# Identity matmuls ahead of the first operands, zero fills on GpSimd, and a later table load in a one-core attention and feed-forward kernel

## The chip, the core and the metric

The kernel runs on one core of a Trainium2 chip. The metric is the device time of one execution in microseconds (us), median of several runs. TensorE does the matmuls, VectorE, ScalarE and GpSimd the work on elements, and SyncE (SP) issues the DMA transfers. Each engine runs its own queue of instructions in order and waits on semaphores for the others. In the profile PE is TensorE, PEld its weight loads, DVE is VectorE, ACT is ScalarE and POOL is GpSimd.

## What is computed

```python
# attention: batch 2, 8 heads, 768 tokens, head size 64, 16 clusters
q_assign = argmax(normalise(q) @ normalise(centroids).T)
k_assign = argmax(normalise(k) @ normalise(centroids).T)
scores = where(q_assign == k_assign, q @ k.T / sqrt(64), -1e9)
attn = softmax(scores) @ v                 # (1536, 512) after the heads are joined
# first feed-forward block, then the second
x = ((x @ w1) * (x @ w2)) @ w3 @ w_out
h = x @ w_in
out = (h * clip(h + 3, 0, 6) / 6) @ w_out2
```

## The kernel before

All operands are float32. To keep their precision on TensorE each one is split into a high part of a shorter format and a low part, and products are made of three matmuls; that is what names like `hi`, `lo`, `woh` and `wol` mean. The weights arrive as 64-bit floating-point numbers and are turned into float32 on the chip, tile by tile: a copy on ScalarE (`cvt`, line 186), a clamp (line 700, mostly on GpSimd) and three integer steps on VectorE (lines 705, 709 and 713: shift, low bits, sign) into `cvs`. From there a tile is either split into `woh` and `wol`, or transposed on TensorE (`pt`, line 731) and split into `wT` (copy on ScalarE, difference on VectorE, line 183). The matmuls `psw` (line 759) multiply weight matrices with each other while attention runs.

There are 16 heads (8 heads in 2 batches). For each head q and k are loaded, split and stacked (`qs`, `ks`), transposed on TensorE (`ptqB`, `ptkB`, line 352) and copied back (`qB`, `kB`). The centroids are normalised once at the start (`cen`, lines 262 to 297, transposed as `pc` and copied to `cT`). The matmuls `pa` (line 378) give each token's products with the 16 centroids; eight small steps (lines 393 to 406, on VectorE and GpSimd) turn them into one-hot codes `ohs`, which TensorE transposes (`pto`, line 367) and which are copied into rows 0 to 15 of `qA` and `kA`. The scores are the sum of two matmuls, `kB` with `qB` and `kA` with `qA` (`pst`, line 484), so that tokens of unlike clusters get a large negative term. Then come the row maximum (line 493), the exponential (line 501), the transposes of the probabilities (`ptr`, line 509) and the product with v (`av`, line 529).

The order on every engine is made before the program is built, by the class `Plan`. Each operation is entered with `op(name, engine, estimated time, function, needs, due=...)`. `order()` walks through them greedily: among the operations that can start soonest on an engine it takes the one that is due first, and it keeps rings of buffers (`take`, `drop`). Operations entered with `fop` have a choice of engine, and the planner gives them to the one that would end first by its estimates. So an operation that is entered, moved or given another time at the start can change the order and the engine of later ones.

At the start four buffers `qA` and `kA` are filled with zeros in rows 0 to 63 (lines 254 and 255). The identity `id_f` is made on GpSimd and cast to `id_r` on VectorE (line 258); every transpose needs one of the two. `cen_2` (line 273) does the square root for the centroids on ScalarE, and with it the one tiny activation that makes ScalarE load the table of the exponential ahead of its first use:

```python
    def cen_2():
        nc.scalar.activation(out=W_["cst"][:, 1:2], in_=W_["cst"][:, 0:1], func=AF.Sqrt)

        nc.scalar.activation(out=W_["warm"], in_=three, func=AF.Exp)
```

Of the kernel before, what the change touches and what calls it, by code (L numbers as in the profile page):

```python
# [8 lines left out]
F32 = mybir.dt.float32  # L9
# [33 lines left out]
class Plan:  # L43
# [10 lines left out]
    def op(self, key, eng, dur, fn, need=(), due=0.0, take=(), drop=(), lat=0.0, lock=False, after=()):  # L54
        assert key not in self.ops, key
        if isinstance(eng, str):
            eng, dur = (eng,), (dur,)
        self.ops[key] = [key, dict(zip(eng, dur)), None, fn, tuple(need), due, tuple(take), tuple(drop), lat,
            len(self.ops), lock, tuple(after)]
# [76 lines left out]
def cluster_attention_moe_kernel(  # L136
# [14 lines left out]
    nc = tc.nc  # L151
# [22 lines left out]
    ps_a = astk.enter_context(tc.tile_pool(name="ps_a", bufs=1, space=PSUM))  # L174
    ps_s = astk.enter_context(tc.tile_pool(name="ps_s", bufs=3, space=PSUM))

    mm = nc.tensor.matmul
# [16 lines left out]
    def blk(i):  # L194
# [15 lines left out]


    NQ, NK, NP, NO = 1, 1, 6, 1
    plan = Plan({
        "raw": 2, "rawx": 6, "cvt": 2, "cvs": 2, "hl": 2, "wT": 3, "m": 1, "s": 3, "r": 2, "a": 1, "x": 1, "x1b": 1,
        "qn": 2, "kn": 2, "vn": 1, "qs": NQ, "ks": NK, "vs": 2, "qB": 2, "kB": 2, "qA": 2, "kA": 2, "oh": NO,
# [3 lines left out]
    op = plan.op  # L219
# [31 lines left out]
    oh_ = [ar.tile([128, NC, 48], F32R, tag=f"oh{i}", name="ohs") for i in range(NO)]  # L251
    for t in oh_:
        nc.gpsimd.memset(t[:, :, NCL:32].bitcast(F32), 0.0)
    for t in (qA_[0], kA_[0], qA_[1], kA_[1]):
        nc.vector.memset(t[0:64].bitcast(F32), 0.0)
    for c in range(NCL):
        nc.gpsimd.memset(wtab[:, c:c + 1], float(NCL - c))
    op("id", "dve", 0.14, lambda: nc.vector.tensor_copy(id_r, id_f), due=-20)

    def cen_load():  # L260
# [12 lines left out]
    def cen_2():  # L273
        nc.scalar.activation(out=W_["cst"][:, 1:2], in_=W_["cst"][:, 0:1], func=AF.Sqrt)

        nc.scalar.activation(out=W_["warm"], in_=three, func=AF.Exp)

    def cen_3():
        cen, csq, cst = W_["cen"], W_["csq"], W_["cst"]
# [15 lines left out]
    def cen_T(s):  # L295
        pt = W_["pc"] = ps_m.tile([128, H, NCL], F32R, tag="m", name="pc")
        nc.tensor.transpose(
            pt.rearrange("p h c -> p (h c)"), W_["cs"][:, s].rearrange("p r d -> p (r d)"), id_r
        )
# [2 lines left out]
    op("cen1", "dve", 0.6, cen_1, ("cenl",), due=-14, take=("as1",))  # L302
    op("cen2", "act", 1.4, cen_2, ("cen1",), due=-13.9)
    op("cen3", "dve", 1.7, cen_3, ("cen2",), due=-13, take=("p",), drop=("p", "as1"))
    op(("cT", 0), "pe", 0.11, lambda: cen_T(0), ("cen3", "id"), due=-10, take=("m",))
    op(("cTc", 0), "dve", 0.2, lambda: nc.vector.tensor_copy(cT[:, :, 0, :], W_["pc"]), (("cT", 0),), due=-9.9,
        drop=("m",))
# [1107 lines left out]
```

## Time and profile before

| | |
|---|---|
| median of 3 runs | 805.14 us (804.45 to 807.4) |
| the profiled execution's own time | 804.47 us |
| its span in the profile | 802.7 us |
| TensorE busy | 770.7 us (96% of the span) |
| VectorE busy | 621.4 us (77%) |
| ScalarE busy | 506.9 us (63%) |
| GpSimd busy | 250.1 us (31%) |

The profile records one execution. Times in the timeline count from the start of the span. A row in the timeline gives the start, the time taken, the engine, the line of the kernel, the operation and its tiles; `x6` says that six like instructions that follow each other stand in one row; in brackets stands how long the engine was idle before it and whose end released it. Matmuls are pipelined, and a row of several runs from the first one's start to the last one's end.

### The profile page before, as it was taken

What the parts mean: (1) busy time and instruction counts of PE and PEld (TensorE: products, weight loads), DVE (VectorE), ACT (ScalarE), POOL (GpSimd) and SP (SyncE); (2) the same over time, 40 slices, a digit from 0 to 9 for tenths busy, and PEclk for the clock granted to TensorE, in tenths of its full rate; (3) what the DMA queues carried; (4) which work ended last, traced back from release to release, by engine and by line L of the source; (5) the groups of instructions that cost most, each with busy time, mean ns of one, the idle gap of its engine ahead of it and who ended that gap; (6) DMA issues with size and microseconds to landing.
All of it is one profiled execution on the core that took longest, in us unless ns stands there. A gap on an engine that the chain in (4) does not pass through costs nothing.

```text
span 802.7 us, 12725 instructions
## 1 busy us (share of the span) xinstructions
PE 770.7 (96%) x4498; PEld 705.8 (88%) x4498; DVE 621.4 (77%) x1095; ACT 506.9 (63%) x1008; POOL 250.1 (31%) x290
## 2 busy tenths in 40 slices
PE   4789999999999999999999999998999999999998
PEld 3677878998889999999889999997889888988986
DVE  7889888899999987788995843779966666766752
ACT  5667877787778776767744532446656557555643
POOL 5654534534355544423221422313121000200000
PEclk9989999999999999999999999999999999999999
DMA  8444333333354543422336587672211213221102
GB/s 274 127 139 127 96 110 86 86 105 110 90 182 136 162 136 109 144 84 83 125 122 186 173 286 258 185 253 96 79 60 61 92 53 132 93 64 57 50 14 78
DMA packets 53135, 98.42 MB, mean 123 GB/s; under 512 B 4848, under 2 KB 31568, under 8 KB 51536
## 3 DMA queue, kind: packets, MB, share of 16 engines
q1 hardware_dynamic: 53072, 97.62, 38.8%
q8 instruction: 35, 0.57, 0.3%
q14 instruction: 28, 0.23, 0.1%
HBM read 73.43 MB, written 17.87 MB: 114 GB/s over the span
## 4 chain that ended last, share of the span: by engine, by line
PE 79%; DVE 7%; ACT 7%; DMA 4%; issue 2%; POOL 0%; SPq 0%; ACTq 0%; DVEq 0%
PE po L1307 15%; PE psh L1263 13%; PE psab L989 8%; PE psx L938 8%; PE psab L821 7%; PE pst L484 7%; PE av L529 6%; PE ptr L509 6%; PE psw L759 4%; PE pa L378 2%; ACT p L501 1%; ACT ph L186 1%; DMA raw<-in_moe_w_dram 1%; DMA qA<-qB 1%; DVE den L493 1%
## 5 line engine op out<-in xcount | busy, mean ns | idle before, releaser
L186 ACT ACTIVATE ph<-ptr 128x384 fp32r<-128x384 f32 x192 | 90.9, 487 | 48.9 <-PE ptr L509 48.1
L183 DVE TENSOR_TENSOR pl<-ptr,ph 128x384 fp32r<-128x384 f32 x192 | 102.7, 549 | 16.3 <-ACT ph L186 15.1
L493 DVE TENSOR_REDUCE den<-pst 128x1 f32<-128x768 f32 x96 | 91.2, 950 | 10.9 <-PE pst L484 8.3
L700 POOL TENSOR_SCALAR cvt<-cvt 128x512 f32<-128x512 f32 x72 | 51.8, 720 | 144.0 <-ACT cvt L186 135.1
L501 ACT ACTIVATE p<-pst,den 128x768 f32<-128x768 f32 x96 | 86.4, 900 | 12.9 <-DVE den L493 12.4
L509 PE MATMUL ptr<-id_f,p 128*128 128x128 f32 x576 | 89.6, 276 | 1.4 <-DVE pl L183 0.7
L821 PE MATMUL psab<-xT,abhl 128*128 128x384 f32 x384 | 85.8, 347 | 0.6 <-ACT asb L186 0.6
L509 PEld LDWEIGHTS ptr<-id_f,p 128*128 128x128 f32 x576 | 69.4, 141 | 9.2 <-PE pt L731 0.9
L186 ACT ACTIVATE cvt<-raw 128x512 f32<-128x512 f32 x72 | 48.1, 669 | 44.1 <-DMA raw<-in_moe_w_out_dram 16.4
L484 PE MATMUL pst<-kB,qB 128*128 128x512 f32 x192 | 71.8, 378 | 3.4 <-ACT p L501 3.1
L529 PE MATMUL av<-ph,vs 128*128 128x384 f32 x192 | 70.2, 366 | 0.1
L529 PE MATMUL av<-pl,vs 128*128 128x384 f32 x192 | 64.9, 338 | 2.1 <-DVE pl L183 2.1
L989 PE MATMUL psab<-xT1s,abhl 128*128 128x384 f32 x384 | 66.9, 334 | 0.0
L989 PEld LDWEIGHTS psab<-xT1s,abhl 128*128 128x128 f32 x384 | 66.5, 188 | 0.2 <-ACT asb L186 0.2
L821 PEld LDWEIGHTS psab<-xT,abhl 128*128 128x128 f32 x384 | 64.7, 188 | 1.9 <-ACT asb L186 0.9
L484 PE MATMUL pst<-kA,qA 128*128 128x512 f32 x192 | 64.9, 342 | 0.2 <-ACT kA L186 0.2
L1285 ACT ACTIVATE tt<-m_sn,three 128x384 f32<-128x384 f32 x48 | 29.4, 616 | 45.9 <-DVE m_sn L1273 34.1
L705 DVE TENSOR_SCALAR cvs<-cvt 128x512 int32<-128x512 int32 x72 | 35.5, 497 | 28.2 <-DMA set<-cvs 21.9
L759 PE MATMUL psw<-woh,wT 128*128 128x512 f32 x128 | 53.3, 428 | 1.0 <-ACT W L186 0.4
L713 DVE SCALAR_TENSOR_TENSOR cvs<-cvt,cvs 128x512 int32<-128x512 int32 x72 | 53.2, 740 | 0.8
L186 ACT ACTIVATE m_sn<-psh 128x384 f32<-128x384 f32 x64 | 31.1, 486 | 33.1 <-PE psh L1263 32.8
L709 DVE SCALAR_TENSOR_TENSOR cvs<-raw,cvs 128x512 int32<-128x512 int32 x72 | 51.2, 714 | 0.9
(184 smaller groups left out, 1832.3 us busy)
## 6 DMA issues: line engine op xcount, KB each, us to landing
raw<-in_moe_w_dram SPq DMA_DIRECT2D x32, 512.0 KB, 3.7
m_gb<-set SPq DMA_DIRECT2D x64, 256.0 KB, 3.4
raw<-in_moe_w_out_dram SPq DMA_DIRECT2D x24, 512.0 KB, 4.9
raw<-in_moe_w_in_dram SPq DMA_DIRECT2D x16, 512.0 KB, 4.2
set<-cvs SPq DMA_DIRECT2D x32, 256.0 KB, 3.5
abp<-abhl SPq DMA_DIRECT2D x6, 1024.0 KB, 4.7
abhl<-abp SPq DMA_DIRECT2D x6, 1024.0 KB, 5.8
qn<-in_q_dram SPq DMA_DIRECT2D x16, 192.0 KB, 2.3
```

What stands on the lines that cost most here:

```text
L183: nc.vector.tensor_tensor(out=out, in0=a, in1=b, op=ALU.subtract)
L186: nc.scalar.activation(out=out, in_=in_, func=AF.Copy, **kw)
L484: x = mm(out=psr[:, t, ks_], lhsT=TT["q" + nm, h][:, i, cs_], rhs=flat(TT["k" + nm, h])[:, ks_], start=st, stop=sp)
L493: done["mx", n] = [other_banks(nc.vector.tensor_reduce(out=dens[h][:, 0, c:c + 1], in_=psS[h, c], axis=AX.X, op=ALU.max, negate=True), ("S ...
L501: done["ex", n] = [other_banks(nc.scalar.activation(out=flat(p), in_=psS.pop((h, c)), func=AF.Exp, bias=d[:, 0, c:c + 1], accum_out=d[:, 1 ...
L509: nc.tensor.transpose(pt[:, blk(c)], pps[h, 3 * hf + c][:, blk(2 * s + i)], id_f)
L529: mm(out=t[:, 0:HF], lhsT=vs_t[h][:, 2 * s + i, :], rhs=x_[:, i, :], start=(s == 0 and i == 0 and n == 0), stop=(s == 2 and i == 1 and n = ...
L759: mm(out=ps, lhsT=wT[m, hf][:, a, blk(kk)], rhs=w_[hf][:, kk, :], start=(g == 0 and n == 0), stop=(g == J1 - 1 and n == 2))
L821: mm(out=ps[:, 0:HF], lhsT=s[:, w, a, blk(kk)], rhs=xT0[0][:, x_, kk, hf * HF:hf * HF + HF], start=(kk == 0 and n == 0), stop=(kk == KD - ...
L989: mm(out=ps[:, 0:HF], lhsT=s[:, w, a, blk(kk)], rhs=x[:, x_, kk, hf * HF:hf * HF + HF], start=(kk == 0 and n == 0), stop=(kk == KD - 1 and ...
L1263: mm(out=ps[:, 0:HF], lhsT=left(p, l, a, kk), rhs=x[:, x_, kk, :], start=(st and kk == 0 and m == 0), stop=(kk == 1 and m == 2), skip_grou ...
L1307: mm(out=outs[b, c], lhsT=g[:, a, blk(c % 3)], rhs=w[:, w_, :], start=(first and a == 0 and w_ == 0), stop=(last and a == 1))
```

## The change

The 36 matmuls multiply the identity with itself into a bank that is used later by `av`; nothing reads them. They are entered as one operation, `idle`, on TensorE, due first of all, and need only `id_r`. The four zero fills are issued on GpSimd and not on VectorE, in the program after the fills of `wtab`. The tiny activation that loads the exponential's table becomes an operation of its own, `table`, which needs the copy of the first head's k (`khi`, 0).

```diff
@@ -210,6 +210,7 @@
 
 
     NQ, NK, NP, NO = 1, 1, 6, 1
+    IDLE0 = 36
     plan = Plan({
         "raw": 2, "rawx": 6, "cvt": 2, "cvs": 2, "hl": 2, "wT": 3, "m": 1, "s": 3, "r": 2, "a": 1, "x": 1, "x1b": 1,
         "qn": 2, "kn": 2, "vn": 1, "qs": NQ, "ks": NK, "vs": 2, "qB": 2, "kB": 2, "qA": 2, "kA": 2, "oh": NO,
@@ -251,10 +252,10 @@
     oh_ = [ar.tile([128, NC, 48], F32R, tag=f"oh{i}", name="ohs") for i in range(NO)]
     for t in oh_:
         nc.gpsimd.memset(t[:, :, NCL:32].bitcast(F32), 0.0)
-    for t in (qA_[0], kA_[0], qA_[1], kA_[1]):
-        nc.vector.memset(t[0:64].bitcast(F32), 0.0)
     for c in range(NCL):
         nc.gpsimd.memset(wtab[:, c:c + 1], float(NCL - c))
+    for t in (qA_[0], kA_[0], qA_[1], kA_[1]):
+        nc.gpsimd.memset(t[0:64].bitcast(F32), 0.0)
     op("id", "dve", 0.14, lambda: nc.vector.tensor_copy(id_r, id_f), due=-20)
 
     def cen_load():
@@ -273,7 +274,15 @@
     def cen_2():
         nc.scalar.activation(out=W_["cst"][:, 1:2], in_=W_["cst"][:, 0:1], func=AF.Sqrt)
 
+    def exp_table():
+
         nc.scalar.activation(out=W_["warm"], in_=three, func=AF.Exp)
+
+    def idle_pe(n):
+
+        t = ps_a.tile([128, 512], F32, tag="a", name="idle")
+        for _ in range(n):
+            mm(out=t[:, 0:128], lhsT=id_r, rhs=id_r, start=True, stop=True)
 
     def cen_3():
         cen, csq, cst = W_["cen"], W_["csq"], W_["cst"]
@@ -302,6 +311,8 @@
     op("cen1", "dve", 0.6, cen_1, ("cenl",), due=-14, take=("as1",))
     op("cen2", "act", 1.4, cen_2, ("cen1",), due=-13.9)
     op("cen3", "dve", 1.7, cen_3, ("cen2",), due=-13, take=("p",), drop=("p", "as1"))
+    op("table", "act", 1.4, exp_table, [("khi", 0)], due=-13)
+    op("idle", "pe", 0.1, lambda: idle_pe(IDLE0), ("id",), due=-30)
     op(("cT", 0), "pe", 0.11, lambda: cen_T(0), ("cen3", "id"), due=-10, take=("m",))
     op(("cTc", 0), "dve", 0.2, lambda: nc.vector.tensor_copy(cT[:, :, 0, :], W_["pc"]), (("cT", 0),), due=-9.9,
         drop=("m",))
```

With these entries the planner makes another order for the first part of the program. On VectorE, `as` are the buffers of the code steps, `cvs` those of the weight tiles and `wT` the split of a transposed weight tile. Before, from the first code step of the first head to its last one on VectorE:

```order
L393 TENSOR_REDUCE as1_259<-pa_238 128x192
L395 TENSOR_REDUCE as2_260<-as1_259 128x12
L705 TENSOR_SCALAR cvs_278<-cvt_231 128x512
L397 TENSOR_TENSOR as1_259<-as1_259,as2_260 128x192
L709 SCALAR_TENSOR_TENSOR cvs_278<-raw_175,cvs_278 128x512
L713 SCALAR_TENSOR_TENSOR cvs_278<-cvt_231,cvs_278 128x512
L395 TENSOR_REDUCE as2_260<-as1_259 128x12
L402 TENSOR_TENSOR ohs_133<-as1_259,as2_260 128x6x16
L705 TENSOR_SCALAR cvs_296<-cvt_263 128x512
L404 TENSOR_TENSOR as1_259<-as1_259,as2_260 128x96
L709 SCALAR_TENSOR_TENSOR cvs_296<-raw6_166,cvs_296 128x512
L183 TENSOR_TENSOR wT_298<-pt_287,wT_298 128x512
```

The same piece with the change:

```order
L404 TENSOR_REDUCE as1_300<-pa_274 128x192
L406 TENSOR_REDUCE as2_301<-as1_300 128x12
L716 TENSOR_SCALAR cvs_310<-cvt_267 128x512
L408 TENSOR_TENSOR as1_300<-as1_300,as2_301 128x192
L720 SCALAR_TENSOR_TENSOR cvs_310<-raw_211,cvs_310 128x512
L724 SCALAR_TENSOR_TENSOR cvs_265<-cvt_235,cvs_265 128x512
L724 SCALAR_TENSOR_TENSOR cvs_310<-cvt_267,cvs_310 128x512
L406 TENSOR_REDUCE as2_301<-as1_300 128x12
L183 TENSOR_TENSOR wT_330<-pt_323,wT_330 128x512
L413 TENSOR_TENSOR ohs_133<-as1_300,as2_301 128x6x16
L716 TENSOR_SCALAR cvs_342<-cvt_321 128x512
L415 TENSOR_TENSOR as1_300<-as1_300,as2_301 128x96
```

The sign step of the first weight tile (`cvs_265`, line 724) now stands inside the code steps; before, it came ahead of them. The difference `wT` now stands ahead of the last three code steps and not behind them.

On GpSimd, `cvt` is the clamp of a weight tile, `qs` and `ks` are the split of the second head's q and k, and `as1` and `ohs` are code steps of the first head. Before, from the first clamp on:

```order
L700 TENSOR_SCALAR cvt_191<-cvt_191 128x512
L189 TENSOR_SCALAR qs_233<-qn_193 128x6x64
L700 TENSOR_SCALAR cvt_231<-cvt_231 128x512
L180 TENSOR_TENSOR qs_233<-qn_193,qs_233 128x6x64
L180 TENSOR_TENSOR wol_254<-cvs_221,woh_253 128x512
L399 TENSOR_TENSOR as1_259<-as1_259,wtab_81 128x192
L700 TENSOR_SCALAR cvt_263<-cvt_263 128x512
L406 TENSOR_SCALAR ohs_133<-as1_259 128x6x16
```

With the change, from the four zero fills on:

```order
L258 MEMSET qA_129 64x768
masks.py:199 AFFINE_SELECT id_f_79<-id_f_79 128x128
L258 MEMSET kA_131 64x768
L711 TENSOR_SCALAR cvt_235<-cvt_235 128x512
L189 TENSOR_SCALAR qs_269<-qn_228 128x6x64
L180 TENSOR_TENSOR qs_269<-qn_228,qs_269 128x6x64
L711 TENSOR_SCALAR cvt_267<-cvt_267 128x512
L189 TENSOR_SCALAR ks_306<-kn_231 128x6x64
L410 TENSOR_TENSOR as1_300<-as1_300,wtab_81 128x192
L180 TENSOR_TENSOR wol_318<-cvs_265,woh_317 128x512
L711 TENSOR_SCALAR cvt_321<-cvt_321 128x512
L417 TENSOR_SCALAR ohs_133<-as1_300 128x6x16
```

Of the four zero fills one stands ahead of the instruction that makes the identity. The second clamp has moved behind both steps on q.

On ScalarE, before, from the first table load on:

```order
L274 ACT_TABLE_LOAD
L274 ACTIVATE cst_169<-cst_169 128x1
L276 ACT_TABLE_LOAD
L276 ACTIVATE warm_159<-three_82 128x1
L186 ACTIVATE qs_177<-qn_162 128x6x64
L186 ACTIVATE ks_189<-kn_164 128x6x64
L186 ACTIVATE cvt_191<-raw6_166 128x512
L186 ACTIVATE qB_212<-ptqB_201 128x384
```

With the change:

```order
L275 ACT_TABLE_LOAD
L275 ACTIVATE cst_206<-cst_206 128x1
L186 ACTIVATE qs_213<-qn_162 128x6x64
L186 ACTIVATE ks_225<-kn_201 128x6x64
L279 ACT_TABLE_LOAD
L279 ACTIVATE warm_159<-three_82 128x1
L186 ACTIVATE cvt_235<-raw6_203 128x512
L186 ACTIVATE qB_248<-ptqB_238 128x384
```

The second table load has moved behind the copies of q and k; the copy of the first weight tile, `cvt`, follows it directly.

## Rows read from the trace of the kernel before

**Rows 1.** Busy time by stretch of 10 us; columns: length, engines, granted clock, DMA share, GB/s.

```profile
30.00:40.00 10.00, 7.39 (x41) 5.80 (x41) 9.89 (x18) 7.68 (x17) 6.82 (x10) 0.86 0.17 55
...
340.00:350.00 10.00, 10.00 (x72) 9.61 (x71) 8.55 (x17) 8.41 (x20) 0.62 (x1) 1.00 0.52 151
```

**Rows 2.** The same view for the two slow stretches and an idle one.

```profile
37.22:40.64 3.42, 2.92 (x15) 2.55 (x13) 3.41 (x7) 2.41 (x6) 3.34 (x6) 0.50 0.17 69
47.46:54.29 6.83, 6.83 (x31) 6.08 (x30) 5.14 (x10) 2.41 (x6) 3.80 (x5) 0.50 0.48 156
...
44.55:46.32 1.77, 0.01 (x1) 0.00 (x0) 1.77 (x5) 1.75 (x5) 1.00 (x2) 1.00 0.84 210
```

**Rows 3.** Timeline of all engines, first 9 us.

```profile
0.99 0.70 DVE L255 MEMSET qA<- 64x768 f32 x1
...
1.18 0.42 SPq L318 DMA_DIRECT2D qn<-in_q_dram  x1
1.62 0.29 POOL masks.py:199 TENSOR_SCALAR_AFFINE_SELECT id_f<-id_f 128x128 f32<-128x128 f32 x1
...
5.01 1.28 ACT L276 ACT_TABLE_LOAD   x1
...
7.57 1.00 PE L352 MATMUL ptqB<-id_r,qs 128*128 128x128 f32 x6 [0.69 <-DVE qs L183]
7.64 0.71 ACT L186 ACTIVATE cvt<-raw 128x512 f32<-128x512 f32 x1 [0.30 <-DMA raw<-in_moe_w_out_dram]
...
8.25 0.85 ACT L186 ACTIVATE qB<-ptqB 128x384 fp32r<-128x384 f32 x2
...
8.37 0.58 PE L352 MATMUL ptkB<-id_r,ks 128*128 128x128 f32 x3
8.43 0.62 POOL L700 TENSOR_SCALAR cvt<-cvt 128x512 f32<-128x512 f32 x1 [6.51 <-ACT cvt L186]
```

**Rows 4.** DMA issues of the page: count, KB each, us from issue to landing.

```profile
qn<-in_q_dram SPq DMA_DIRECT2D x16, 192.0 KB, 2.3
```

**Rows 5.** Timeline: the last transposes, the shift, the centroid matmuls of two heads.

```profile
8.88 0.58 PE L352 MATMUL ptkB<-id_r,ks 128*128 128x128 f32 x3
...
9.08 0.43 DVE L705 TENSOR_SCALAR cvs<-cvt 128x512 int32<-128x512 int32 x1 [0.90 <-POOL cvt L700]
...
9.86 1.43 PE L378 MATMUL pa<-cT,qB 128*128 128x32 f32 x6 [0.40 <-DVE cT L309]
...
11.13 1.44 PE L378 MATMUL pa<-cT,kB 128*128 128x32 f32 x6
...
23.83 0.82 PE L378 MATMUL pa<-cT,kB 128*128 128x32 f32 x6
```

**Rows 6.** Timeline of VectorE, 12 to 17 us.

```profile
12.61 0.56 DVE L393 TENSOR_REDUCE as<-pa 128x192 f32<-128x384 f32 x1 [1.39 <-PE pa L378]
...
14.37 0.68 DVE L709 SCALAR_TENSOR_TENSOR cvs<-raw,cvs 128x512 int32<-128x512 int32 x1
...
15.08 0.96 DVE L713 SCALAR_TENSOR_TENSOR cvs<-cvt,cvs 128x512 int32<-128x512 int32 x1
...
16.34 0.29 DVE L402 TENSOR_TENSOR ohs<-as,as 128x96 fp32r<-128x96 f32 x1
...
16.89 0.25 DVE L404 TENSOR_TENSOR as<-as,as 128x96 f32<-128x96 f32 x1
```

**Rows 7.** Timeline: GpSimd's q steps, the weight tile's transposes and difference, the first scores.

```profile
9.82 0.86 POOL L189 TENSOR_SCALAR qs<-qn 128x384 fp32r<-128x384 f32 x1 [0.77 <-DVE cT L309]
...
11.66 0.99 POOL L180 TENSOR_TENSOR qs<-qn,qs 128x384 fp32r<-128x384 f32 x1
...
16.19 1.09 PE L731 MATMUL pt<-id_f,cvs 128*128 128x128 f32 x4 [2.48 <-DVE cvs L713]
...
17.94 0.69 DVE L183 TENSOR_TENSOR wT<-pt,wT 128x512 fp32r<-128x512 f32 x1 [0.20 <-ACT wT L186]
...
19.95 0.63 PE L484 MATMUL pst<-kB,qB 128*128 128x512 f32 x1
```

## Prediction

> **What bounds the kernel now.** I first read the table of busy time by stretch. From 340 to 350 us TensorE is busy for all 10.00 us: there a delay or a gain that reaches TensorE goes straight into the total. From 30 to 40 us it is VectorE that is full (9.89 of 10) while TensorE has 7.39 [rows 1]. So the change is decided in the first 60 us, and the question is when the first head's scores start, because from then on VectorE and afterwards TensorE have no slack to make up for a late start. The planner's order is the same again from TensorE's instruction 1,080 on, about a quarter of the program.
>
> Next I read the timeline of the first 24 us for the chain that leads to the first scores at 19.95: ScalarE copies the transposed q (8.25), TensorE multiplies with the centroids (9.86 to 12.57), VectorE and GpSimd turn that into codes (on VectorE 12.61 to 17.14), TensorE transposes the codes and the scores start [rows 3, 5, 6, 7].
>
> TensorE's granted clock has to be read with care. The column says 0.50 for 37.22 to 40.64 and for 47.46 to 54.29 and 1.00 between them, at 44.55, as at the start [rows 2]. But at 7.57 six transposes need 1.00 us, and six of the narrow centroid matmuls need 1.43 to 1.44 us at 9.86 and 11.13, against 0.82 us at 23.83 [rows 3, 5]. [...]
>
> **The change, part by part.** *Table load.* The exponential's table load (1.28 us at 5.01) goes behind the copies of q and k. That would bring q's transposes forward. But on ScalarE's row the next item before the copies of qB is the copy cvt of the first weight tile, and it waits until 7.64 for the DMA that brings that tile, with 0.30 us of idle time in front [rows 3]. That transfer is unchanged on SP. So qB is copied at 8.25 in either kernel: gain 0. The cost if the cover fails: q is issued at 1.18 and such loads land 2.3 us after issue [rows 3, 4], so 3.5; then the copies and the table load are over before 7.64. Only if q landed as late as the trace allows, right behind that load (6.3), would the moved load push cvt back: 6.3, two copies of 0.43 us (half of 0.85) and 1.28 make 8.4, 0.8 us late. I take 0.
>
> *Memsets.* Four of 0.70 us leave VectorE, where they end before the centroid work begins [rows 3]. GpSimd gets them; no row has one of this size there, so 0 below and 0.93 above (the 0.62 us of the clamp at 8.43, 512 columns, times 768/512). I take 0.7, near VectorE's price. One now stands ahead of the select that makes the identity, at 1.62 with 0.29 us, so the identity is ready at about 2.6. The other three end by 5.7 at the most, and GpSimd's first clamp is at 8.43 [rows 3]: cost 0. VectorE's centroid work can start about a microsecond earlier, which meets the same wall at 7.64.
>
> *The 36 matmuls.* From 7.57 to 8.37, where the next transposes start, six cost 0.80 us, 0.133 each [rows 3]. 36 make 4.8 us, from about 2.9 to 7.7 at the lower clock, less if it rises on the way. q's transposes then start at 7.85 instead of 7.57, still mostly in the shadow of cvt: 0 to 0.3 us. They may lift the clock for the centroid matmuls pa, which is their only direct use.
>
> *What the planner moves.* This is where I see the price. pa can begin when the last of k's transposes are done, 9.46 (8.88 + 0.58). k's second copy moves to VectorE behind the shift L705, which ends at 9.51; with half of 0.85 us it is ready at about 10.0 [rows 3, 5]. At the higher clock pa then ends at about 11.05 (0.82 us for the second six), at the lower at 12.2 (9.46 + 1.27 + 1.44). Before it was 12.57. So 0.4 to 1.5 us are won here.
>
> They are lost again on VectorE. Before, L393 at 12.61 is followed by L709 at 14.37, 1.76 us on; the same three steps lie between them now, so L720 starts 1.76 us after pa, at 12.86 to 13.96. (The clamp of that tile now stands behind both q steps on GpSimd, 0.86 and 0.99 us; with its 0.62 it ends between 11.5 and 12.3, and is wanted at 12.0 at the earliest) [rows 3, 6, 7]. Then 0.71 us, and now **two** sign steps L724 of 0.96 us where there was one, because the first tile's was put off: 15.49 to 16.59. The transposes pt follow 0.15 us later, as they do now (16.04 to 16.19): 15.64 to 16.74. And then comes the new wait: the difference wT, which needs pt and its copy and started 1.75 us after pt (16.19 to 17.94), now stands **ahead** of the three code steps; before, they ran in that gap. VectorE, which is in order, sits idle until wT starts at 17.39 to 18.49; it takes 0.69 us, and the code steps 0.80 us (16.34 to 17.14) [rows 6, 7]. They end at 18.88 to 19.98 instead of 17.14: 1.7 to 2.8 us late. Queued behind them are GpSimd's last code step, the code transposes and the scores. Behind that the three psw matmuls have gone ahead of the code transposes and one ScalarE copy of weights has come between two code copies; I count the two against each other. Over the whole program the planner also gives ScalarE five small copies that VectorE had, some 0.43 us each; behind 60 us they lie beside TensorE's work, so 0, at best -2.1 us.
>
> Which end? The 36 matmuls are dense for longer than any stretch of the first 12 us now, so I take the higher clock for pa, and add 0.3 us for a clamp that comes late because GpSimd does both q steps first: **+2.0 us**; ends +1.7 and +3.1 (with the 0.3 of the burst). [...]
>
> *Sum.* The profiled execution took 804.47 us (span 802.7), 0.67 below the median of the three runs, 805.14, and at their lower edge. 804.47 + 2.0 = **806.5**.
>
> **The rivals.** *Late end.* The burst does not do what it says: the clock is not up, or not any more, when pa runs. Then pa keeps its 1.44 us and the sum is +3.1: 807.6. For it: pa comes 1.8 us after the burst. Against: nothing in the rows.
>
> *Absorbed.* The wait in front of wT is not real, because VectorE gets the sign steps done in time, or other idle time takes it up: 804.5. Against it: VectorE is full from 30 us on [rows 1].
>
> *Faster.* The clock stays up, or the moved order closes the gaps before the two slow stretches. In those TensorE was busy 2.92 and 6.83 us at half rate [rows 2]; at full rate they would take half, -1.5 and -3.4. 806.5 - 4.9 = 801.6, and 799.6 if the 2.0 us are absorbed as well; 800.6 lies between. For it: in the new order three psw matmuls stand in front of the third head's pa, where TensorE idled. Against: before the slow stretch at 47.46 TensorE had idled 1.77 us from 44.55 on [rows 2], and nothing in the change makes its releasers there faster.
>
> *Slower.* The new wait makes the gaps before the first scores longer, and TensorE falls once more, or rises one stretch later. A stretch like the second costs half of 6.83 us, 3.4: 806.5 + 3.4 = 809.9. It is decided in TensorE's gap before psw, which VectorE's wait for wT lengthens: after 1.77 us without work from 44.55 on, the clock fell [rows 2].
>
> **How the numbers follow.** Forecast 0.36 (805.5 to 807.3); late end 0.13; absorbed 0.11; faster 0.24 (799.5 to 802.5); slower 0.16 (808.8 to 811). About 0.5%, 4 us, is what a measurement of this kernel can tell from no change: 801.1 to 809.2 against the median. Below lie two thirds of the faster rival, 0.16. Above lie most of the slower one and the tail of the late end, 0.15. The rest, 0.69, is no change. The range 800.6 to 809.8 leaves out half of the faster rival and half of the slower one, 0.2.
>
> **What would show it.** Right: cvt still starts near 7.6 and qB near 8.3; pa ends near 11; VectorE idle for a microsecond or more in front of the wT difference; the first scores near 22. Wrong: cvt well before 7.6 (then the table load did count); VectorE with no gap before wT, or scores before 20; a clock column without the two stretches at 0.50, which would be the faster rival; or a third one, the slower.

## The result, and the profile after

The change makes the kernel slower: 813.69 us, median of 6 runs (812.84 to 818.42), against 804.92 us (803.27 to 807.58, also 6). The ratio is 1.0109 [1.0083, 1.0134]: 8.8 us more, outside the predicted range and more than four times the predicted loss of 2.0 us. The profiled execution took 813.35 us (span 811.5); TensorE is busy 780.4 us of it, 9.7 more than before, of which the 36 matmuls are 7.94.

The timeline of the changed kernel, rows of TensorE, VectorE, ScalarE and GpSimd up to the point where TensorE's 512-column matmuls first take 0.40 us:

```profile
2.61 1.41 DVE L259 CAST id_r<-id_f 128x128 fp32r<-128x128 f32 x1 [1.75 <-POOL id_f masks.py:199]
...
3.20 0.73 POOL L258 MEMSET qA<- 64x768 f32 x1
...
4.07 7.94 PE L285 MATMUL idle<-id_r 128*128 128x128 f32 x36 [4.07 <-DVE csq L270]
...
7.43 0.67 ACT L186 ACTIVATE cvt<-raw 128x512 f32<-128x512 f32 x1 [0.36 <-DMA raw<-in_moe_w_out_dram]
...
11.94 0.96 PE L363 MATMUL ptqB<-id_r,qs 128*128 128x128 f32 x6
...
12.56 0.87 ACT L186 ACTIVATE qB<-ptqB 128x384 fp32r<-128x384 f32 x2 [4.47 <-PE ptqB L363]
...
13.88 1.43 PE L389 MATMUL pa<-cT,qB 128*128 128x32 f32 x6
...
15.15 1.44 PE L389 MATMUL pa<-cT,kB 128*128 128x32 f32 x6
...
18.70 1.68 DVE L724 SCALAR_TENSOR_TENSOR cvs<-cvt,cvs 128x512 int32<-128x512 int32 x2
...
22.27 0.69 DVE L183 TENSOR_TENSOR wT<-pt,wT 128x512 fp32r<-128x512 f32 x1 [1.64 <-ACT wT L186]
...
23.38 0.25 DVE L415 TENSOR_TENSOR as<-as,as 128x96 f32<-128x96 f32 x1
...
26.30 0.76 PE L495 MATMUL pst<-kB,qB 128*128 128x512 f32 x1
...
33.72 0.63 PE L495 MATMUL pst<-kA,qA 128*128 128x512 f32 x1
...
34.99 0.40 PE L495 MATMUL pst<-kA,qA 128*128 128x512 f32 x1
```

The same cast of the identity in the kernel before:

```profile
4.04 0.15 DVE L258 CAST id_r<-id_f 128x128 fp32r<-128x128 f32 x1
```

The first row of the changed kernel's timeline is the identity's cast, 0.15 us long before and 1.41 here, beside the zero fills on GpSimd. The burst starts at 4.07, takes 7.94 us (0.22 each) and ends at 12.0. ScalarE's copy cvt starts at 7.43, where the prediction had it [rows 3], but qB comes at 12.56, 4.3 us late, and ScalarE has idled 4.47 us for it. The six transposes right behind the burst take 0.96 us, against 1.00 before [rows 3], and the centroid matmuls pa take 1.43 and 1.44 us as before [rows 5]: the burst has not lifted the clock. pa ends at 16.59 instead of 12.57. VectorE then waits 1.64 us in front of wT; the code steps end at 23.63 instead of 17.14 [rows 6], and the first scores start at 26.30 instead of 19.95 [rows 7]: 6.35 us late, 4.0 at pa's end and 2.3 from there on.

The last two rows of that timeline answer a question that the prediction asked too early: when does TensorE's clock rise? A 512-column matmul takes 0.63 us at the lower level and 0.40 at the higher; neighbours overlap and start 0.43 and 0.23 us apart. With the change they take 0.63 until 33.7, more than 7 us behind the first scores. Before, the six pa matmuls at 23.83 already took 0.82 [rows 5], 3.9 us behind the first scores. Busy time of the changed kernel in three stretches (columns as in [rows 1]):

```profile
26.30:34.55 8.25, 8.23 (x31) 6.91 (x31) 4.44 (x8) 3.60 (x8) 4.09 (x6) 1.00 0.67 197
44.75:51.75 7.00, 6.00 (x26) 5.37 (x26) 6.95 (x15) 4.22 (x9) 4.37 (x7) 0.51 0.13 39
340.00:350.00 10.00, 10.00 (x71) 9.59 (x70) 7.83 (x14) 7.72 (x19) 3.82 (x4) 1.00 0.50 181
```

In the first, TensorE works 8.23 us at the lower level (512 columns at 0.63 us) while the column says 1.00: it does not record the start. In the second, the only recorded slow stretch, there are 6.00 us, against the two of before, 2.92 and 6.83 [rows 2]. From 340 to 350 us nothing has changed: TensorE is full [rows 1].

### The profile page after: what moved, and what is told of

Read it like the earlier page. It is cut to its first block, busy times and chain, and to the rows that moved or that the text cites. A ratio compares the mean times of both kernels' runs of the same rounds, so it can differ in the third digit from the quotient of the medians.

```text
span 811.5 us, 12799 instructions
## 1 busy us (share of the span) xinstructions
PE 780.4 (96%) x4534; PEld 712.6 (88%) x4534; DVE 618.1 (76%) x1086; ACT 508.5 (63%) x1014; POOL 251.4 (31%) x293
## 4 chain that ended last, share of the span: by engine, by line
PE 70%; DVE 11%; DMA 8%; ACT 6%; issue 3%; POOL 1%; SPq 0%; DVEq 0%; ACTq 0%; POOLq 0%
PE po L1318 15%; PE psh L1274 13%; PE psab L832 7%; PE pst L495 7%; PE av L540 6%; PE ptr L520 6%; PE psw L770 4%; PE psab L1000 3%; DMA set<-cvs 2%; PE pa L389 2%; PE psx L949 2%; DMA m_gb<-set 2%; DVE cvs L720 1%; DMA raw<-in_moe_w_dram 1%; PE idle L285 1%
## 5 line engine op out<-in xcount | busy, mean ns | idle before, releaser
L711 POOL TENSOR_SCALAR cvt<-cvt 128x512 f32<-128x512 f32 x72 | 49.9, 694 | 148.4 <-ACT cvt L186 139.0
L520 PEld LDWEIGHTS ptr<-id_f,p 128*128 128x128 f32 x576 | 69.2, 141 | 11.4 <-ACT qB L186 1.2
```

The costliest lines, as they stand in the source:

```text
L520: nc.tensor.transpose(pt[:, blk(c)], pps[h, 3 * hf + c][:, blk(2 * s + i)], id_f)
```

## The experiments

All of them were timed in five rounds against the kernel before (its median in these comparisons lay between 804.93 and 805.61), apart from the two second profiles. A ratio is to the kernel before, with its 95% interval in brackets; it can differ a little from the quotient of the two medians.

### Which part costs

The burst alone, in the order of before (it is issued with the identity's cast, so that the planner does not see it):

```diff
-    op("id", "dve", 0.14, lambda: nc.vector.tensor_copy(id_r, id_f), due=-20)
+    def id_and_idle():
+        nc.vector.tensor_copy(id_r, id_f)
+        t = ps_a.tile([128, 512], F32, tag="a", name="idle")
+        for _ in range(36):
+            mm(out=t[:, 0:128], lhsT=id_r, rhs=id_r, start=True, stop=True)
+
+    op("id", "dve", 0.14, id_and_idle, due=-20)
```

> The 36 matmuls alone, issued right behind the cast of the identity, in the order of before on every engine. Theory A (the burst is too long: 36 matmuls take 7.9 us and end near 12, so everything that waits for TensorE starts some 4 us late): first centroid matmuls near 13.9 instead of 9.86, first scores near 24.2 instead of 19.95, total 808.5 to 811. Theory B (the order that the planner makes is what costs; the burst lies beside the loads): total 804 to 806. Theory C (the clock: the burst lifts it, and what is lost is lost later): centroid matmuls at 0.8 us for six.

Measured: 810.27 us, 1.0067 [1.0045, 1.0089]. Its timeline:

```profile
4.24 7.94 PE L262 MATMUL idle<-id_r 128*128 128x128 f32 x36 [4.24 <-DVE id_r L259]
...
14.05 1.43 PE L384 MATMUL pa<-cT,qB 128*128 128x32 f32 x6
...
23.97 0.63 PE L490 MATMUL pst<-kB,qB 128*128 128x512 f32 x1
...
26.32 0.39 PE L490 MATMUL pst<-kA,qA 128*128 128x512 f32 x1
```

The burst's late end (12.2) is handed on almost whole: pa 4.2 us late, the first scores 4.0.

All three edits in the order of before (the burst as above, the fills on GpSimd, the table load behind the first copy of k):

> All three edits, but in the order of before on every engine. Theory A: burst from 4.1 to 12, first scores near 24.2, total 808.5 to 811, as with the burst alone. Theory B: total 804 to 806. If zero fills and table load gained anything by themselves, this is below the burst alone by that.

Measured: 809.62 us, 1.0067 [1.0042, 1.0093], first scores at 23.79. The other two edits add nothing to the burst that can be told. They were then tried without it, same order:

```diff
-    for t in (qA_[0], kA_[0], qA_[1], kA_[1]):
-        nc.vector.memset(t[0:64].bitcast(F32), 0.0)
...
+    for t in (qA_[0], kA_[0], qA_[1], kA_[1]):
+        nc.gpsimd.memset(t[0:64].bitcast(F32), 0.0)
...
-        nc.scalar.activation(out=W_["warm"], in_=three, func=AF.Exp)
...
+        if h == 0:
+            nc.scalar.activation(out=W_["warm"], in_=three, func=AF.Exp)
```

> The zero fills on GpSimd and the later table load alone, in the order of before, without the identity matmuls. Theory that both are worth nothing, because the copy cvt waits for its transfer until about 7.5 in any case: q's copy qB at 8.1 to 8.3, first scores at 19.7 to 20.0, the time within 0.2% of before. Rival, that they gain the 0.7 us that VectorE is relieved of: 804.2 us. Rival, that the cast of the identity, which took 1.41 us beside GpSimd's fills, costs: identity at 4.0 as before, so nothing as well; a loss would show as a start of the first scores after 20.5.

Measured: 805.77 us, 1.0009 [0.9992, 1.0025], no difference that can be told.

```profile
2.61 1.40 DVE L258 CAST id_r<-id_f 128x128 fp32r<-128x128 f32 x1 [1.75 <-POOL id_f masks.py:199]
...
7.26 0.68 ACT L186 ACTIVATE cvt<-raw 128x512 f32<-128x512 f32 x1 [0.21 <-DMA raw<-in_moe_w_out_dram]
7.85 0.85 ACT L186 ACTIVATE qB<-ptqB 128x384 fp32r<-128x384 f32 x2
```

cvt still waits for its transfer, as predicted. The identity is ready at 4.01 although VectorE has no fill in front of it: the cast is held up beside GpSimd's fills.

The changed kernel without the burst, `IDLE0 = 0`, and with the order alone (also the fills and the table load undone, the entries for the planner kept):

> The changed kernel without the 36 matmuls, order otherwise as in the change. Theory A: first scores near 22 instead of 26.3, total 808 to 810, 4 to 6 under the change. Theory B: total 812 to 814, as the change.

> The order of the change alone: no burst, zero fills on VectorE, table load where it was. Theory A and my forecast's step (code steps 1.7 to 2.8 us late): first scores near 22, total 805.5 to 808.5, and within 1 of the kernel without the burst. Theory B: total 812 to 814. If the later order is harmless: 804 to 806.

Measured: 809.05 us, 1.0060 [1.0040, 1.0080], and 810.37 us, 1.0063 [1.0043, 1.0082]. The first of the two:

```profile
8.98 1.43 PE L389 MATMUL pa<-cT,qB 128*128 128x32 f32 x6
10.25 1.44 PE L389 MATMUL pa<-cT,kB 128*128 128x32 f32 x6
...
17.38 0.69 DVE L183 TENSOR_TENSOR wT<-pt,wT 128x512 fp32r<-128x512 f32 x1 [1.64 <-ACT wT L186]
...
18.48 0.25 DVE L415 TENSOR_TENSOR as<-as,as 128x96 f32<-128x96 f32 x1
...
21.40 0.76 PE L495 MATMUL pst<-kB,qB 128*128 128x512 f32 x1
...
30.48 0.48 PE L495 MATMUL pst<-kA,qA 128*128 128x512 f32 x1
30.80 0.39 PE L770 MATMUL psw<-woh,wT 128*128 128x512 f32 x1
```

So the loss has two parts of about the same size that add up within their intervals: the burst 0.67%, the new order 0.60%, both 1.09%. The new order's code steps end at 18.73 and its first scores are only 1.45 us late, but the kernel loses 0.60%, more than 4 us; and the higher clock comes at 30.7.

### How the burst costs

Half the burst in the changed kernel, `IDLE0 = 18`:

> The changed kernel with 18 identity matmuls in place of 36; order of every engine unchanged. By the full burst's row (7.94 us for 36) 18 take 4.0 us, from 4.07 to 8.0. Theory that only the part of the burst that reaches past q's transposes counts (they start at 6.99 without a burst): about 1.2 us late, the first scores at 22.6 instead of 21.4, and 810.3 us (809.05 without a burst, plus 1.2). Rival, that each of the matmuls costs the same wherever it ends: half of the way from 809.05 to 813.69, 811.4 us. Rival, that a burst costs by its being there (its bank, its wait): 813 us.

Measured: 809.36 us, 1.0053 [1.0041, 1.0065], which cannot be told from the kernel without a burst (809.05, 1.0060). The burst runs from 4.07 to 8.2 (4.11 us), and the first scores start at 22.45, 1.05 us later than without it. Half the matmuls do not cost half the loss (811.4): what counts is where the burst ends.

The same number of columns in nine wide matmuls, in the order of before:

```diff
-        for _ in range(36):
-            mm(out=t[:, 0:128], lhsT=id_r, rhs=id_r, start=True, stop=True)
+        for _ in range(9):
+            mm(out=t, lhsT=id_r, rhs=id_r.unsqueeze(1).to_broadcast([128, 4, 128]), start=True, stop=True)
```

> The order of before, with the identity matmuls as 9 of 512 columns in place of 36 of 128: the same number of columns. Theory that the 0.22 us of a narrow one is the price of the instruction with its own load of weights: 9 take 0.43 us each (the 512-column matmuls psw have a mean of 0.43), 3.9 us, from 4.24 to 8.1, the first scores at 20.5 and the time 805.5 us. Rival, that it is the price of the columns: 0.86 us each, 7.7 us in all, and 810 us as with the narrow ones. Rival on the clock: these do lift it, and the six matmuls pa take 0.82 us instead of 1.43; then the first scores come 1.2 us earlier than by the rest, at 19.3, and the time is 804.3 us.

Measured: 805.52 us, 1.0011 [0.9994, 1.0028]. Two readings of this kernel, its timeline:

```profile
4.24 3.92 PE L262 MATMUL idle<-id_r 128*128 128x512 f32 x9 [4.24 <-DVE id_r L259]
...
8.06 0.65 PE L358 MATMUL ptqB<-id_r,qs 128*128 128x128 f32 x6
...
9.53 0.81 PE L384 MATMUL pa<-cT,qB 128*128 128x32 f32 x6
...
19.45 0.63 PE L490 MATMUL pst<-kB,qB 128*128 128x512 f32 x1
```

and the busy time behind it:

```profile
8.00:11.00 3.00, 2.90 (x27) 2.56 (x25) 2.48 (x5) 2.28 (x6) 1.88 (x3) 1.00 0.67 241
11.40:21.20 9.80, 5.86 (x28) 4.83 (x28) 8.18 (x16) 4.96 (x10) 8.48 (x10) 0.50 0.94 320
```

The same columns take half the time, 3.92 us against 7.94: on average 0.22 us for one of 128 columns and 0.44 for one of 512, so the price of a narrow one is that of the instruction, not of its columns. And these nine do lift the clock: the six transposes right behind them take 0.65 us and pa 0.81 us for six, where the 36 narrow ones left them at 0.96 and 1.43. It falls again by 11.4, behind transposes and pa that kept TensorE busy for 2.90 of the 3 us from 8 to 11, and now the column shows 0.50 while a 512-column matmul takes 0.63: what the prediction read from row times alone, that the start runs at the lower level and the column leaves it out, is shown. The scores run at the lower level again, and the time is that of before.

The changed kernel with this burst, `IDLE0 = 9` and the same two lines:

> The changed kernel, all three edits and its order, with the identity matmuls as 9 of 512 columns, which took 3.92 us in the order of before and lifted the clock (six pa in 0.81 us). Theory that the narrow burst costs by ending late and by not lifting the clock: this burst runs from 4.07 to 8.0, pa takes 0.8 us for six, the first scores come 1.2 us before the 22.45 of the half burst, at 21.2, and the time is that of the new order without a burst, 808.8 us (808 to 810): the new order's part of the loss stays. Rival, that the new order is late only while TensorE's clock is low at the start: 805 to 806 us. Rival, that any burst adds to the new order: 811 us or more.

Measured: 808.31 us, 1.0034 [1.0020, 1.0047]. The burst runs from 4.07 to 8.3, pa takes 0.81 us, the first scores come at 21.85 (0.65 later than expected), and the clock, which fell by 12.5, rises again only at 36. More than half of the change's loss went with the shape of 36 matmuls.

The burst entered with the time that it takes:

```diff
-    op("idle", "pe", 0.1, lambda: idle_pe(IDLE0), ("id",), due=-30)
+    op("idle", "pe", 7.9, lambda: idle_pe(IDLE0), ("id",), due=-30)
```

> The changed kernel with the operation of the 36 identity matmuls entered at 7.9 us, which they take, and not at 0.1. The planner then moves weight steps of VectorE ahead of the first code steps; every engine is otherwise nearly as in the change. Theory that the end of the burst at 12.0 sets the start of the chain whatever the order: pa as in the change (13.9), but the code steps have less between them (one sign step less, two other steps less), so the first scores come about 1.5 us earlier, at 24.8, and the time is 812.2 us. Rival, that the wrong entry of 0.1 us is what costs: the burst's part (4.6 us) and the order's go, 807 us. Rival, that the place of the steps does not matter: 813.5 us.

Measured: 812.30 us, 1.0072 [1.0050, 1.0095], first scores at 24.50 and 512 columns at 0.40 from about 27. A planner that knows the time fills it with other steps, but what waits for TensorE still waits. The pauses of TensorE behind psw are as long here as in the change (0.48 us before the code transposes, 0.62 before ptkB), only the one in front of pt is shorter (1.28 us instead of 3.09), and yet the clock rises about 2.5 us behind the first scores and not 8.

### How the new order costs

The difference wT behind the code steps again (on `new_order_no_burst`):

```diff
             op(("wtl", m, hf), "dve", 0.6, lambda m=m, hf=hf: w3_lo(m, hf), (("wth", m, hf),), due=d - 0.3,
-                drop=("s",))
+                drop=("s",), after=(("oh6", 0),) if m + hf == 0 else ())
```

> The new order without the identity matmuls (809.05 us), with one thing put back: the difference wT stands behind the first head's code steps again. Theory that the wait in front of wT is what makes the new order late: VectorE's idle time of 1.64 us and the 0.69 us of wT leave the code steps' path, the first scores at 19.1 instead of 21.4, and the time 2.3 us less, 806.8 us. Rival, that the new order loses its time later (transfers of abhl and m_sn that TensorE waits for): the first scores move as said, and the time stays at 808.5 to 809.5 us.

Measured: 808.57 us, 1.0044 [1.0030, 1.0058], which cannot be told from 809.05, and the first scores did not move:

```profile
8.29 0.66 ACT L186 ACTIVATE cvt<-raw 128x512 f32<-128x512 f32 x1 [1.23 <-DMA raw<-in_moe_w_out_dram]
...
16.59 1.23 DVE L413 TENSOR_TENSOR ohs<-as,as 128x96 fp32r<-128x96 f32 x1
...
19.11 0.83 PE L378 MATMUL pto<-id_r,ohs 128*48 128x128 f32 x6 [1.59 <-POOL ohs L417]
...
21.46 0.76 PE L495 MATMUL pst<-kB,qB 128*128 128x512 f32 x1
...
23.47 0.39 PE L495 MATMUL pst<-kA,qA 128*128 128x512 f32 x1
```

This expectation failed. The planner moved more than wT: the order differs on every engine. 0.8 us of the miss is this execution's own: the transfer in front of cvt landed late (8.29, against 7.21 in the profile without this edit), and pa starts at 9.80 instead of 8.98. The rest was lost again in the order: the wait is gone, but the code step L413 takes 1.23 us (16.59 to 17.82) instead of 0.25 beside a GpSimd step (wol, 16.43 to 17.71); GpSimd's last code step stands behind a clamp; and the three psw matmuls, which ran in the wait, stand between the code transposes and the scores. What did move is the clock: psw now stands close before the scores, and 512 columns take 0.39 us from 23.5 on. Part of that was given back later: from 29.75 to 36.75 the column says 0.51, with 6.15 us of work.

That made the late clock the suspect. Seven wide identity matmuls were put into the pause of TensorE in front of the transposes pt, without the burst and in the change itself:

```diff
     def w3_T(m, hf):
+        if m + hf == 0:
+            t = ps_a.tile([128, 512], F32, tag="a", name="fill")
+            for _ in range(7):
+                mm(out=t, lhsT=id_r, rhs=id_r.unsqueeze(1).to_broadcast([128, 4, 128]), start=True, stop=True)
```

> The new order without the burst (809.05 us), and 7 matmuls of 512 columns on the identity between the transposes of the second head's q (end at 12.5) and the transposes pt of the weight tile (15.62), where TensorE has nothing to do: 7 of 0.43 us, 3.0 us, in 3.1. Nothing else moves. Theory that the new order is dear because TensorE's clock rises late, at about 30.7, 9.2 us behind the first scores, where in the order of before it rises at 22.75, 2.8 us behind: with the gap filled the first scores run at the higher clock (0.40 for 512 columns instead of 0.63) or reach it by 24; TensorE's 9.29 us of work from 21.40 to 30.70 lose half, less the 1.4 us that before loses as well, so 3 us, and the time is 806 us (805 to 807). Rival, that TensorE's clock there is covered by VectorE: the scores run faster, and the time stays at 808.5 to 809.5. Rival, that the clock rises late in any case: 512 columns at 0.63 until 30, 809 us.

> The changed kernel (813.69 us) with the same 7 wide matmuls between the second head's q transposes (end at 17.4) and pt (20.52), 3.0 us in a gap of 3.1. Theory of the late rise: the first scores still at 26.3, since the burst is unaltered, but at the higher clock or reaching it by 29 instead of 34.5; of TensorE's 8.23 us from 26.30 to 34.55 half goes, less 1.4, so 2.7 us: 811 us (810 to 812). What is left over 805 is then the burst's 4 us and the later start of the new order. Rival, covered by VectorE: 813 to 814.5 us. Rival, that the clock rises late in any case: 813.7 us with 512 columns at 0.63 until 34.

Measured: 808.64 us, 1.0031 [1.0005, 1.0057], and 814.08 us, 1.0111 [1.0096, 1.0126]. Both leave the question open, and the second missed its 811 us. The clock rose (psw takes 0.40 us), but fell behind two pauses of 0.90 us at the code transposes and ptkB, and stayed low longer. The first of the two kernels:

```profile
16.00:22.00 6.00, 3.04 (x18) 1.72 (x17) 4.51 (x10) 3.77 (x8) 4.31 (x5) 1.00 0.98 372
22.25:35.90 13.65, 13.18 (x47) 10.52 (x46) 10.25 (x15) 8.04 (x17) 8.50 (x10) 0.50 0.33 102
```

So every pause up to the second head's scores was filled: 7 in front of pt, 2 in front of psw, 3 in front of the code transposes, 3 behind them, 4 behind the second head's pa, the order of every engine otherwise unchanged.

> The new order without the burst (809.05 us) with wide identity matmuls in each of TensorE's pauses up to the second head's scores: 7 in front of pt, 2 in front of psw, 3 in front of the code transposes, 3 behind them, 4 behind the second head's pa. With the first seven alone the clock rose before pt and fell again at about 22.3, behind pauses of 0.90 us in front of the code transposes and in front of ptkB, and stayed low until about 36; the time was 808.64. Theory that the low clock behind the first scores is a good part of what the new order loses: with the pauses filled it stays up through the scores (512 columns at 0.40 us from 18 to 30), TensorE's work of 9.3 us that the new order does there at half rate is 3 to 4.5 us shorter, and the time is 806 us (805 to 807). Rival, that VectorE or ScalarE covers it: the scores run at 0.40, first scores as late as before or later, and the time stays at 808.3 to 809.5. Rival, that fillers in front of waiting work cost as much as they give: 810 us.

Measured: 807.59 us (801.81 to 810.01, 12 runs), 1.0017 [0.9997, 1.0038], against 1.0060 [1.0040, 1.0080] with the pauses. The median is 1.6 us above what was expected.

```profile
20.82 0.46 PE L506 MATMUL pst<-kB,qB 128*128 128x512 f32 x1
21.12 0.41 PE L506 MATMUL pst<-kA,qA 128*128 128x512 f32 x1
...
25.55 0.40 PE L506 MATMUL pst<-kB,qB 128*128 128x512 f32 x1
```

The clock stays up from pt (four transposes in 0.63 us at 15.63) to 29; from 29.00 to 32.75 the column says 0.54. By the ratios 0.43 of the 0.60% are gone, by the medians about half (2.0 us above the kernel before instead of 4.1). The profiled run is the fastest of the twelve (801.81), so its rows are not those of the median run.

How much of that is the clock can be looked at behind 200 us, where TensorE's order is the same in all versions. The same score matmul in the kernel before, the new order without the burst, the same with the pauses filled, and the change with the wide burst:

```profile
205.00 0.46 PE L484 MATMUL pst<-kB,qB 128*128 128x512 f32 x1
207.84 0.46 PE L495 MATMUL pst<-kB,qB 128*128 128x512 f32 x1
202.60 0.46 PE L506 MATMUL pst<-kB,qB 128*128 128x512 f32 x1
209.01 0.46 PE L495 MATMUL pst<-kB,qB 128*128 128x512 f32 x1
```

The new order is 2.84 us late here, 1.45 of it already at the first scores, so about half of the delay arises on the way, where the clock is low. But the last kernel speaks against a simple account: its clock rises even later (at 36 instead of 30.7) and it is 4.01 us late here, and yet its time, 1.0034 [1.0020, 1.0047], is not above the 1.0060 of the new order without a burst. And why the clock stays low is open as well: without the burst TensorE works 9.29 of the 9.30 us from 21.40 to 30.70, with no pause to speak of, before it rises. That the late clock is a part of the new order's cost is shown by the filled pauses; how large a part is not shown.

The same idea in the order of before, nine wide matmuls at the start and six in the pause in front of pt:

> The order of before with the 9 wide matmuls at the start (805.52 us) and 6 more of 512 columns between the second head's q transposes (end near 13.3) and pt (16.1): 2.6 us at the lower clock in a gap of 2.8. Theory that TensorE's clock at the start is worth time: pa at 0.8 us for six, the weights' and the first scores' 512 columns at 0.40 us instead of 0.63 from 18.6 on, the first scores at 19.0 instead of 19.95 and 1.4 us less for what before does at the lower clock behind them: 2 us less than before, 803 us, a ratio of 0.9975. Rival, that VectorE covers it: 805 to 805.5 us and a ratio of 1.000. Rival, that six more delay pt: 806.5 us.

Measured: 804.39 us, 0.9989 [0.9975, 1.0004], where 803 was expected; first scores at 19.16 and at 0.40 us. It is the only version that is not above the kernel before, by less than can be told from nothing.

### What scatters by itself

> The changed kernel unaltered, for a second profile. Theory that the start repeats and the later part scatters: the first scores at 26.2 to 26.4 again; the number of stretches at the lower clock and the waits of TensorE for abhl and m_sn differ from the first profile's (one stretch of 6.8 us, 2.1 and 1.5 us), by 1 to 3 us. Rival, that the later waits belong to the order: abhl 2 us again.

> The kernel before unaltered, for a second profile. Theory that the start repeats and the later part scatters: first scores at 19.9 to 20.0, two stretches at the lower clock of 10.2 us together give or take one of 3.4 us, waits of TensorE behind 330 us of 4 to 8 us in all. Rival, that the first profile's 802.7 us is what this order always gives: all of these within 0.3 us of the first profile.

The second profile of the change took 817.44 us, that of the kernel before 808.20. The starts repeat: 26.29 and 20.09 for the first scores. Behind them the kernel before differs from itself: waits of TensorE from 330 us on (us in total, times, longest; abhl and m_sn are tiles of the feed-forward blocks) in its second profile,

```profile
PE psh L1263 <- ACT m_sn L186: 2.7, 3, 1.7
PE psab L989 <- DMA abhl<-abp: 1.8, 2, 1.0
```

where the first had 1.2 us for m_sn and none for abhl, and the change in its first profile

```profile
PE psab L1000 <- DMA abhl<-abp: 2.1, 3, 0.8
PE psh L1274 <- ACT m_sn L186: 1.5, 3, 0.8
```

A late wait for a transfer looked like a cost of the change when one profile was laid beside one. The second profiles do not settle it: abhl costs the change 2.1 us in both, as the rival said, and the kernel before none and 1.8. The recorded slow stretches scatter likewise: one of some 7 us in the change's first profile, two of some 10 us together in its second.

## Why the prediction was wrong

**The 36 matmuls: wrong, and this is the step that failed.** It took 0.133 us each from six transposes and let them run from 2.9 to 7.7, hidden by cvt, for 0 to 0.3 us. Measured: 0.22 us each and 4.07 to 12.0, for 5.3 us (the burst alone against before). Of the 4.3 us at the end, 3.1 are the length and 1.2 the start. The row was of another instruction: the transposes' weights load in 0.82 us for six, 0.137 each, while the burst's 36 loads take 7.75 us in the row of loads that belongs to it, 0.215 each, so the loads fill it:

```profile
4.07 7.75 PEld L285 LDWEIGHTS idle<-id_r 128*128 128x128 f32 x36 [4.07 <-DVE csq L270]
```

The trace of before had rows of the right kind. The transposes that the prediction went by, and pa, whose six matmuls of 32 columns load 128x128 weights each:

```profile
7.57 0.82 PEld L352 LDWEIGHTS ptqB<-id_r,qs 128*128 128x128 f32 x6 [0.88 <-DVE qs L183]
...
9.82 1.35 PEld L378 LDWEIGHTS pa<-cT,qB 128*128 128x128 f32 x6 [0.55 <-ACT kB L186]
```

pa's loads take 0.225 us each, and its two groups of six start 1.27 us apart (9.86 and 11.13 [rows 5]), 0.21 each. 36 at these prices make 7.6 to 8.1 us; 7.94 were measured. The prediction read pa's rows for the clock alone. The step also rested on a wall (cvt at 7.6) that hides anything up to 7.6 and nothing beyond; the upper end of its own bound, 7.7, was already there. The half burst shows the wall: with an end at 8.2 its time cannot be told from that without a burst.

**The identity at 2.6: right for `id_f`, wrong for `id_r`.** The memsets take 0.73 us on GpSimd as guessed and `id_f` is ready at 2.58, but the cast to `id_r` beside them takes 1.41 us, so that it ends at 4.02, against 4.19 before. The cast ends right behind the end, at 3.93, of the second of GpSimd's fills that run beside it (3.20 + 0.73); what holds it up there is not shown. The step had counted the fills as free once they were off VectorE.

**Table load and fills worth nothing: right**, by the run of the two without the burst in the order of before (1.0009 [0.9992, 1.0025]), by the three edits against the burst alone (both 1.0067), and by the new order with and without the two (1.0060 and 1.0063); and for the reason given, the transfer in front of cvt.

**The clock: half right.** That the start runs at the lower level behind a column of 1.00 is shown by the wide burst (512 columns take 0.63 us at 19.45, where the column says 0.50). That the burst, being dense, would lift it for pa was the author's estimate, and the +2.0 us rest on it; no run shows 0.82 us for pa behind the 36. TensorE worked 7.94 us without a break and pa took 1.43 us all the same, while nine of 512 columns, 3.92 us, did lift it (pa at 0.81). Behind the wide burst the clock fell again by 11.4, after transposes and pa; no run separates the two. The late-end rival, with pa at its 1.44 us, had this right and priced it at 1.1 us.

**The planner's order: right on the way, too small at the end.** Without the burst pa ends 0.9 us earlier (predicted 0.4 to 1.5), VectorE waits 1.64 us in front of wT (predicted over 1), the code steps end at 18.73, 1.6 us late (1.7 to 2.8), and the scores start 1.45 us late. The prediction carried this 1:1 to the end. Measured is 0.60%, 4.8 us by the ratio and 4.1 by the medians. The step from first scores to the end failed: it did not ask what the new order does to TensorE's clock there. The slower rival did, with "rises one stretch later" as one of its two ways, at 3.4 us, and gave it 0.16; filling the pauses gave back 0.43%, 3.5 us (2.1 by the medians). Nor is the wait for wT alone the cause of the late scores: without it, and with the late transfer taken off, they would have come 0.8 us earlier, of 2.3 expected.

**Slower, same or faster:** the direction of the forecast was right, but the chance of more than 0.5% was put at 0.15, because the two sizes above were small. Still open is why the clock rises so late in the new order, and how much of that order's cost is the clock: 1.0017 [0.9997, 1.0038] does not settle whether any cost remains with the clock up, and the change with the wide burst lost no more than the new order alone although its clock rose later.

## What to carry to other kernels

A filler is free only up to the wall that hides it: price it from its own kind of instruction (a matmul with its weight load, not a transpose), take the later of its possible starts, and leave room to the wall. If it is there for the clock, look in the rows behind it whether it lifts the clock at all and how long the clock stays up. A reorder near the start should be followed past its first result, to where TensorE's matmuls take their short time and to where both orders are the same again; and one profile beside one does not tell a late wait for a transfer from scatter.

## What was not expected of the hardware

- 36 matmuls of 128 columns in 7.94 us without a break leave the clock at its lower level (pa at 1.43 us for six); 9 of 512 columns in 3.92 us lift it (0.81).
- A cast of 128x128 on VectorE takes 1.41 us instead of 0.15 while GpSimd fills memory (1.40 in the run with fills and table load alone).
- In the runs here the recorded clock column agrees with row times only after its first change in a run: 0.63 us for 512 columns under 1.00 in most kernels here, under 0.50 where wide matmuls had lifted it earlier, as at 19.45 in the run with the wide burst.
- Keeping the clock up through the first scores of before, by estimate 1.4 us of work less (half, by the column's 0.50 for rows of 0.63 us, of the 2.80 us that TensorE works from 19.95 to 22.75), moves the median from 805.28 to 804.39 us, which cannot be told from nothing.
